# Batch 0 loaded in four row pieces and folded over d only; two thirds of the weight folding placed between FFN steps

## The chip, the cores and the metric

The kernel runs on one core of a Trainium2 chip. The time is the device time of a whole execution in microseconds (us). Runs of one kernel spread, and the profiled run is one of them (for the kernel before, it is one more, of 707.55 us).

Engine names in the profile: PE is TensorE, PEld its weight loads, DVE VectorE, ACT ScalarE, POOL GpSimd, SP the engine that issues most DMAs. "L434" is line 434 of that kernel's file, so the same instruction has another line number in another kernel.

## The reference

```python
def reference(x, w_gate, w_val, w_out):          # x (8, 3008, 256), weights 256 -> 1536 -> 256
    X = np.fft.fft(np.fft.fft(x, axis=1), axis=2).real.astype(np.float32)
    t = X.reshape(8 * 3008, 256)
    gate = np.maximum(t @ w_gate, 0.0)
    return (gate * (t @ w_val) @ w_out).astype(np.float32)
```

The kernel does the Fourier transform over the sequence in two matrix stages (3008 = 94 x 32) and puts the transform over d = 256 into the FFN weights ("weight fold": cosine and sine tables times the raw weights, 12 pieces of 512 columns, in fp32). Symmetry halves the work: rows j and 32-j, and columns d and 256-d, are first added and subtracted ("fold"), and the FFN of a mirrored position is had from the same products with one more term ("mirror").

The FFN is a chain of steps t = 0 to 287: 8 batches x 3 blocks x 12 column tiles f, 36 steps a batch. While the FFN of batch b runs, stage 1, a shuffle through DRAM, rotate and stage 2 of batch b+1, and load and fold of batch b+2, are slipped in at given steps.

## The kernel before

The load and the fold of one batch. A fold is a chain of small instructions on one engine; in the FFN loop GpSimd gets one of them per step (three in batch 0).

```python
def load_x(b, q):
    xl = xp.tile([NA, J, D], F32, tag="xl")             # one buffer each: the next load waits
    xh = xp.tile([96, NB // 2, D], F32, tag="xh")       # for the end of this fold
    for p0, n in ((0, 80), (80, 14)):
        q.dma_start(out=xl[p0:p0 + n], in_=...)
    nc.gpsimd.indirect_dma_start(out=xh[:]..., ...)     # the mirrored rows, gathered
...
def fold(b, eng, lo, hi):                               # chunks of up to 3 row pairs
    ...
    yield lambda: eng.tensor_tensor(c1, x1, rev, op=ALU.subtract)
    yield lambda: eng.tensor_tensor(x1, x1, rev, op=ALU.add)
    yield lambda: eng.tensor_tensor(e1[:, :, H + 1:D], ...)
    yield lambda: eng.tensor_tensor(e1[:, :, 1:H], ...)

def fold_all(b, eng):                                   # 23 fold steps
    for lo in range(1, J - 1, XC):
        yield from fold(b, eng, lo, min(lo + XC, J - 1))
    yield from fold_ends(b, eng)
    yield from fold_edges(b, eng, 0, J)                 # columns 0 and 128, once, at the end
```

The start: tables, the fold of batch 0 on DVE and GpSimd, stage 1, the shuffle, all weight folds, stage 2.

```python
load_x(0, nc.sync)
# ... the raw weights, 3 MB, in four loads right behind it; sine tables on DVE, ACT, POOL ...
for lo, hi in ((2, 5), (5, 8), (8, 10), (10, 12)):
    run(fold(0, nc.vector, lo, hi)); ...
for lo, hi in ((12, 14), (14, 16)):
    run(fold(0, nc.gpsimd, lo, hi))
...
for k, c in enumerate((1, 2, 3, 4, 5, 6, 7, 0)):
    stage1(0, c, "dve" if k in (5, 7) else "act")
for k in (2, 4, 6, 0):
    shuffle_out(0, k, k + 2)
load_x(1, nc.scalar)
...
for blk in range(NBLK):
    shuffle_in(0, 4 * blk, 4 * blk + 4)
run(fold_all(1, nc.gpsimd))
for n in range(DF // 512):
    for i in range(2):
        for cs in range(2):
            ...                                         # one weight fold: 2 fp32 matmuls 128x512 (psw)
rotate(0)
for blk in range(NBLK):
    stage2(0, blk, 0, "act"); stage2(0, blk, 1, "dve")
```

One FFN step. In a "split" step (two of three, from batch 1 on) the mirror product h is made by GpSimd, in the others by DVE. `gs` and `gm` share one pool of five buffers; GpSimd's mirror product is what frees `gm`. The names in the profiles: G and V are the gate and value products on TensorE, `gs` and `gm` the rectified gate of a position and of its mirror, E what DVE prepares for GpSimd's mirror product; `psw` is the product of a weight fold, `eo` the result of the fold, `pq` that of stage 2, `psr` that of rotate.

```python
gp = ctx.enter_context(tc.tile_pool(name="gp", bufs=5, space=SB))
def split(t):
    return NBLK * NF <= t < len(steps) and t % 3 != 2
...
def mirror_h(t, eng, val):
    eng.tensor_tensor(free(e["h"][:], ...), e["gm"][:]..., val[:]..., op=ALU.mult)
...
tl, tf, t1, tr, d2 = (17, 18, 16, 28, 1) if b == 0 else (1, 8, 6, 22, 2)   # load, fold, stage 1, rotate
```

## Time and profile before

| | before |
|---|---|
| time, median of 3 runs | 707.9 us (706.92 to 708.68) |
| span of the profiled run | 705.8 us |
| PE busy | 646.8 us (92%) |
| first G matmul of the FFN | 71.32 us |
| first gs ACTIVATE | 72.44 us |
| a step of batch 0: steps 0 to 11, 12 to 35 | 1.81, 2.42 us |
| a batch of 36 steps, batches 1 to 5 | 77.4 us |
| batch 6, which loads and folds nothing | 76.9 us |

A "batch" here is the time from the gs ACTIVATE of its first step to that of the next batch's first step.

First the chain of waits of the first 74 us: start, length, what. It names at each moment the work that everything later waited for.

```profile
1.73 18.37 DMA xh<-in_x_dram,ix
20.12 0.96 DVE xc L98
...
32.45 0.42 DVE xl L99
...
33.53 1.27 POOL xc L98
...
40.71 0.68 POOL eo L102
...
44.10 22.21 PE psw L346 x48
...
70.57 0.70 DVE pq L180
71.32 0.61 PE G L390
```

The start is one serial chain: 18 us for the gathered rows, DVE's fold, then GpSimd's two chunks alone until 41.4, stage 1, and 22 us of weight folding on TensorE. The shuffle of batch 0 is slow, too: the waits of the SP queue show (engine, line, for what: total, times, longest)

```profile
SPq L157 <- DMA Td<-t_282: 15.5, 1, 15.5
```

because it runs beside the loads of batch 1 and `w_out`. The Trainium skill ("DMA: Bandwidth & Descriptors", "Issuing engines are not separate DMA queues") says that DMAs of all issuing engines run on the same 16 DMA engines and interleave; the trace agrees: the wait was 15.5 us beside these loads. It cost nothing, as the weight fold hid it.

In the first 12 FFN steps TensorE has gaps. PE's part of the timeline, one step: start, duration, what, and in brackets the idle time before it and what ended that.

```profile
83.51 0.38 PE L434 MATMUL V<-pq,wm_91 128*128 128x512 bf16 x1 [0.37 <-DVE h L411]
83.72 0.38 PE L407 MATMUL V<-pq,wc_87 128*128 128x512 bf16 x1
83.94 0.38 PE L409 MATMUL V<-pq,ws_89 128*128 128x512 bf16 x1
84.16 0.38 PE L397 MATMUL G<-pq,wm_90 128*128 128x512 bf16 x1
84.37 0.38 PE L390 MATMUL G<-pq,wc_86 128*128 128x512 bf16 x1
84.58 0.38 PE L391 MATMUL G<-pq,ws_88 128*128 128x512 bf16 x1
85.33 0.38 PE L434 MATMUL V<-pq,wm_91 128*128 128x512 bf16 x1 [0.37 <-DVE h L411]
```

Six matmuls start 0.215 us apart and fill 1.29 us of a step of 1.82; the durations of 0.38 overlap. So each of these steps has 0.53 us of room. Later steps also carry the output matmuls, and TensorE is full: in batch 3 (busy time of each engine and number of instructions, windows view)

```profile
307.08:384.47 77.39, 76.46 (x516) 50.25 (x525) 62.78 (x97) 52.18 (x100) 59.97 (x49) 1.00 0.43 108
```

PE is busy 76.46 of 77.39 us; the columns after PE are PEld, DVE, ACT and POOL, then the clock, DMA share and GB/s.

### The profile page before, as it was taken

The numbers are of one execution on the slowest core, as the hardware profiler recorded it, in microseconds if no ns is written. First come the engines' busy times: TensorE is split into PE (matmuls) and PEld (weight loads), VectorE is DVE, ScalarE is ACT, GpSimd is POOL, SyncE is SP. The second block draws the span as 40 slices with busy tenths as digits, with TensorE's granted clock in tenths as the row PEclk, the third lists the DMA queues.
The fourth block names the chain that finished last, engine by engine and source line by source line (L and its number), as shares of the span: only waits on it lengthen the run. The fifth ranks groups of instructions, "written<-read, shape, count | busy, mean of one in ns | idle before, by whom it ended". The sixth has DMA issues, their size and how long they took to land.

```text
span 705.8 us, 12357 instructions
## 1 busy us (share of the span) xinstructions
PE 646.8 (92%) x4198; PEld 415.8 (59%) x4276; DVE 519.0 (74%) x830; ACT 428.5 (61%) x798; POOL 448.3 (64%) x393
## 2 busy tenths in 40 slices
PE   0169899899999999999999999999999999999997
PEld 0024356566666666666666666666666666666665
DVE  6712665568888878787888788888878888888881
ACT  2114557567666676667666766667676766665662
POOL 2845918915996499847995599747994334434341
PEclk9999999999999999999999999999999999999999
DMA  9458081573511932265413842185221151111213
GB/s 203 179 133 162 23 181 35 158 185 69 147 37 46 214 110 80 62 143 133 123 38 88 200 118 58 46 179 141 80 59 53 31 148 37 57 50 29 59 30 89
DMA packets 30480, 70.81 MB, mean 100 GB/s; under 512 B 4264, under 2 KB 21184, under 8 KB 28224
## 3 DMA queue, kind: packets, MB, share of 16 engines
q1 hardware_dynamic: 27844, 55.01, 29.6%
q0 software_dynamic: 2448, 13.37, 9.0%
q10 hardware_dynamic: 124, 1.64, 1.0%
q8 instruction: 33, 0.54, 0.3%
q14 instruction: 31, 0.25, 0.1%
HBM read 39.83 MB, written 30.96 MB: 100 GB/s over the span
## 4 chain that ended last, share of the span: by engine, by line
PE 72%; POOL 12%; issue 5%; DVE 4%; DMA 4%; ACT 1%; SPq 0%; DVEq 0%; POOLq 0%
PE po L452 28%; PE G L391 8%; PE V L409 7%; PE G L397 7%; PE V L407 6%; POOL h L423 6%; PE G L390 6%; PE V L434 3%; PE psw L346 3%; DMA xh<-in_x_dram,ix 3%; POOL xl L99 2%; POOL xc L98 2%; POOL eo L102 1%; DVE h L411 1%; POOL eo L100 1%
## 5 line engine op out<-in xcount | busy, mean ns | idle before, releaser
L423 POOL TENSOR_TENSOR h<-gm,E 128x512 bf16<-128x512 f32 x168 | 213.9, 1273 | 190.5 <-DVE E L431 169.9
L452 PE MATMUL po<-wo,h 128*128 128x256 bf16 x2304 | 324.2, 272 | 1.6
L452 PEld LDWEIGHTS <-h 128*128 128x128 bf16 x2304 | 222.6, 98 | 86.6 <-issue 10.8
L400 ACT ACTIVATE gm<-G 128x512 f32<-128x512 f32 x288 | 172.6, 599 | 140.1 <-PE G L397 140.1
L411 DVE TENSOR_TENSOR h<-gs,V 128x512 bf16<-128x512 f32 x288 | 190.3, 684 | 51.0 <-PE V L409 47.7
L392 ACT ACTIVATE gs<-G 128x512 f32<-128x512 f32 x288 | 171.8, 596 | 5.3 <-POOL h L423 3.0
L423 DVE TENSOR_TENSOR h<-gm,V 128x512 bf16<-128x512 f32 x120 | 82.6, 688 | 75.2 <-ACT gm L400 52.6
L417 DVE SCALAR_TENSOR_TENSOR E<-nb,af,V 128x512 f32<-128x512 bf16 x168 | 125.3, 746 | 7.0 <-PE V L407 3.6
L431 DVE SCALAR_TENSOR_TENSOR E<-E,V 128x512 f32<-128x512 f32 x168 | 114.3, 680 | 0.0
L397 PE MATMUL G<-pq,wm_90 128*128 128x512 bf16 x288 | 109.4, 380 | 2.2 <-ACT gs L392 2.1
L391 PE MATMUL G<-pq,ws_88 128*128 128x512 bf16 x287 | 109.0, 380 | 2.3
L409 PE MATMUL V<-pq,ws_89 128*128 128x512 bf16 x280 | 106.2, 379 | 0.1
L407 PE MATMUL V<-pq,wc_87 128*128 128x512 bf16 x263 | 100.0, 380 | 0.2 <-issue 0.2
L455 ACT COPY os<-po 128x512 f32<-128x512 f32 x96 | 56.2, 586 | 67.9 <-PE po L452 67.9
L390 PE MATMUL G<-pq,wc_86 128*128 128x512 bf16 x244 | 93.0, 381 | 0.8 <-DVE pq L180 0.8
L98 POOL TENSOR_TENSOR xc<-xl,xh 94x768 f32<-94x768 f32 (+1 forms) x37 | 66.0, 1784 | 34.7 <-DMA xh<-in_x_dram,ix 18.0
L99 POOL TENSOR_TENSOR xl<-xl,xh 94x768 f32<-94x768 f32 (+1 forms) x37 | 66.0, 1782 | 1.7
L434 PE MATMUL V<-pq,wm_91 128*128 128x512 bf16 x120 | 45.5, 379 | 3.9 <-DVE h L411 3.9
L409 PEld LDWEIGHTS <-ws_89 128*128 128x128 bf16 x288 | 28.2, 98 | 34.2 <-issue 0.3
L391 PEld LDWEIGHTS <-ws_88 128*128 128x128 bf16 x288 | 28.2, 98 | 34.0 <-issue 0.3
L134 PEld LDWEIGHTS <-w_81 94*96 94x96 bf16 x120 | 15.6, 131 | 50.1 <-issue 27.0
L407 PEld LDWEIGHTS <-wc_87 128*128 128x128 bf16 x288 | 28.2, 98 | 22.1 <-issue 7.5
(349 smaller groups left out, 393.7 us busy)
## 6 DMA issues: line engine op xcount, KB each, us to landing
out_dram<-os SPq DMA_DIRECT2D x176, 128.0 KB
xl<-in_x_dram SPq DMA_DIRECT2D x7, 1360.0 KB
nb<-Nd SPq DMA_DIRECT2D x24, 128.0 KB
xl<-in_x_dram SPq DMA_DIRECT2D x7, 238.0 KB
wst_108<-in_moe_w_gate_dram SPq DMA_DIRECT2D x2, 768.0 KB
wst_111<-in_moe_w_val_dram SPq DMA_DIRECT2D x2, 768.0 KB
out_dram<-os SPq DMA_DIRECT2D x16, 96.0 KB
xl<-in_x_dram ACTq DMA_DIRECT2D x1, 1360.0 KB
```

Source lines behind the costliest of these rows:

```text
L390: nc.tensor.matmul(e["G"][:], lhsT=wc[0][:, fs], rhs=pq[:, 0, :], start=True, stop=False)
L391: nc.tensor.matmul(e["G"][:], lhsT=ws[0][:, fs], rhs=pq[:, 1, :], start=False, stop=True)
L392: nc.scalar.activation(e["gs"][:], e["G"][:], ACTF.Relu)
L397: nc.tensor.matmul(e["G"][:], lhsT=wm[0][:, f * 128:(f + 1) * 128], rhs=pqt[b, blk][:, 1, :], start=False, stop=True, skip_group_check=True)
L400: nc.scalar.activation(e["gm"][:], e["G"][:], ACTF.Relu)
L407: nc.tensor.matmul(e["V"][:], lhsT=wc[1][:, fs], rhs=pq[:, 0, :], start=True, stop=split(t))
L409: nc.tensor.matmul(e["V"][:], lhsT=ws[1][:, fs], rhs=pq[:, 1, :], start=False, stop=True, skip_group_check=split(t))
L411: nc.vector.tensor_tensor(e["h"][:, 0, :], e["gs"][:], e["V"][:], op=ALU.mult)
L417: nc.vector.scalar_tensor_tensor(e["E"][:], nbt[b, blk][:], af[:, f:f + 1], e["V"][:], op0=ALU.mult, op1=ALU.add)
L423: eng.tensor_tensor(free(e["h"][:], 512 + NB - 1, [NB, 16], [-1, NB]), e["gm"][:].rearrange("p (a k) -> p a k", k=NB), val[:].rearrange("p ...
L431: nc.vector.scalar_tensor_tensor(e["E"][:], e["E"][:], 2.0, e["V"][:], op0=ALU.mult, op1=ALU.subtract)
L452: nc.tensor.matmul(po[:, s % 2, :], lhsT=ht[t - f + ff]["h"][:, sg, g * 128:(g + 1) * 128], rhs=wo[:, ff, :], start=(ff == 0), stop=(ff == ...
```

## The change

Intent: shorten the start. Batch 0 comes in four row pieces on one queue, alone; each piece is folded over d as soon as it is there, and the mirrored rows are not added by DVE but by a second matmul in stage 1, with its own table `w1h`. The raw weights come in thirds, into buffers that `h` uses later; one third is folded before the FFN, the others at steps 0 to 7, where TensorE has room. The loads of batch 1 are issued after the shuffle. Because batch 1 comes later, the plan of loads, folds and stages moved, and GpSimd's mirror products start 8 steps later.

```diff
+    FIRST = (0, 24, 8, 16)
+    def load_first():
+        ...
+        for r in FIRST:
+            nc.sync.dma_start(out=(xl if r < 16 else xh)[:, r % 16:r % 16 + 8, :],
+                              in_=view(x, r * D, [[NB * D, 96], [1, 8 * D]]))
+    def fold_first(r):                       # over d only: two tensor_tensors of 94 x 8 x 127, one copy
+        ...
     def stage1(b, c, evac):
...
-            if jj:
+            if jj and b == 0:
+                nc.tensor.matmul(o, lhsT=w1[:, jj, :], rhs=eo[:, jj, :], start=True, stop=False)
+                nc.tensor.matmul(o, lhsT=w1h[:, NB // 2 - jj, :], rhs=eh[:, NB // 2 - jj, :], start=False, stop=True)
+            elif jj:
...
     def fold(b, eng):                        # now 22 fold steps
...
+            eng.tensor_copy(free(e1, 0, [D, n], [H, 2]), free(x1, 0, [D, n], [H, 2]))   # edges, in each chunk
...
-        yield from fold_edges(b, eng, 0, J)
...
+        for blk in range(NBLK):
+            shuffle_in(0, 4 * blk, 4 * blk + 4)
+        load_w(1)
+        load_w(2)
...
+        nc.gpsimd.tensor_copy(si[0:1, 0:1], wst[1, 2, 1][0:1, 0:1])   # holds batch 1's gather back
+        load_x(1, nc.sync)
...
+        for i in range(2):
+            for cs in range(2):
+                fold_w(0, i, cs)
...
-        return NBLK * NF <= t < len(steps) and t % 3 != 2
+        return NBLK * NF + 8 <= t < len(steps) and t % 3 != 2
...
+    for k in range(4):
+        at(k, fold_w, 1, k // 2, k % 2)
+        at(4 + k, fold_w, 2, k // 2, k % 2)
+        at(8 + k, stage2, 0, 1 + k // 2, k % 2, "dve")
+    # load, fold, stage 1, shuffle, rotate, stage 2
+    plan = {0: (28, 34, (14, 16, 18, 19, 21, 23, 24, 25), 26, 33, (33, 34, 36, 38, 40, 42)),
+            1: (12, 19, range(11, 19), 19, 26, (26, 27, 29, 31, 33, 35)),
+            2: (7, 13, range(6, 14), 14, 22, (23, 25, 27, 29, 31, 33))}
...
-            for fn in itertools.islice(folds[0], 3 if t < NBLK * NF else 1):
+        for k in range(2 if t < NBLK * NF + 8 else 1):
+            while folds and next(folds[0], folds) is folds:
```

## The prediction

> **What bounds it now.** Two regimes. From the end of the prologue on, TensorE is the limit: the windows view gives PE busy 197.4 us in 200:400 and 197.8 in 400:600 at clock 1.00, and successive gs ACTIVATEs are 2.15 us apart on average. Before that is a serial prologue of 71.3 us (first G matmul in the timeline at 71.32). The chain of waits through it: the gather of xh lands at 20.1 (18.4 us, beside xl and the 3 MB of raw weights); DVE folds to 33.3; POOL folds alone 33.5 to 41.5; stage 1 ends at 44.1; the 48 fp32 weight-fold instructions hold PE to 66.3 (22.2 us; the first four 0.85 us each, then 0.43); stage 2 and its evictions to 71.3.
>
> **What the change does.**
> - Batch 0 arrives as four 0.79 MB pieces, alone at first. At the 190 to 260 GB/s of the first microseconds I estimate landings near 5.5, 9, 12.5 and 16 us.
> - DVE builds a table twice as wide (94x1536; from 1.00 us for a 94x816 tensor_tensor I estimate 1.9, all of it done near 8 us), then folds each piece in two tensor_tensors of 94x1016 (about 1.1 us each, from 0.4 per 381 elements) plus edges: 2.5 us a piece, last done near 18.5. The row fold (and POOL's 8 us) is gone; 15 extra 94x256 matmuls come, about 0.2 us each.
> - Stage 1 then ends near 23.5 and the shuffle is no longer behind batch 1's loads. Now shuffle_in waits 15.5 us for it (waits of the SP queue), hidden under the weight fold. The Trainium skill, "DMA: Bandwidth & Descriptors", section on issuing engines, says queues interleave on the same 16 engines; the trace agrees, and the change issues batch 1's load after the shuffle. I expect t4 near 31.
> - One third of the weight fold stays: 16 instructions, about 8.5 us with the cold start, near 25.5 to 34. First gs near 37.5 instead of 72.4: 35 us saved.
> - Given back: 8 folds of 1.72 us between steps 0 to 7. These steps take 1.82 us now with 6 matmuls of 0.215, so 0.5 us of each is PE slack; with the fold they become PE-bound at 3.0. Steps 8 to 11 carry stage 2, about 2.1. Block of 12: 32.5 instead of 21.7 us, +10.8.
> - Steps 36 to 43 become unsplit (6 value/gate matmuls, 2.4 against 2.16 us) and take stage 2 of batch 1: +2.5. The 4.2 us step of batch 0 (rotate waiting for its DMA) should vanish: -1.5. POOL's backlog near step 44, where the mirror products start behind fold 2: +0.5.
>
> **Sum.** 707.9 - 35 + 10.8 + 2.5 - 1.5 + 0.5 = about 685 us (-3.2%). Range 679 to 692. Faster by over 2% 0.93, within 2% 0.06, slower 0.01.
>
> **What would show it.** First gs at 35 to 40 us; wait of stage 1 on the last piece, not on POOL; steps 0 to 7 at about 3.0 us with PE busy throughout; steps 12 to 35 near 2.35 us; unchanged 2.15 us in batches 2 to 7.
>
> **What would make it wrong.** The pieces landing late (then the first gs slips one for one); shuffle_in taking much more than 5 us; the raw weights of the other thirds landing after steps 0 to 4 need them; batch 1's fold on POOL (from near 55 us, 29 us long) arriving late for stage 1 at step 14; a POOL backlog at step 44 that stalls E and gs buffers for several us.

## The result

| | before | after |
|---|---|---|
| time, median (4 runs each) | 708.06 us | 690.98 us (690.47 to 693.31) |
| ratio, 95% interval | | 0.9767 (0.9741 to 0.9793) |
| span of the profiled run | 705.8 us | 688.8 us |
| PE busy | 646.8 us (92%) | 653.0 us (95%) |
| first gs ACTIVATE | 72.44 us | 36.56 us |

Ratios are the mean time of one kernel's fast runs over the mean of the other's of the same rounds, so not quite the ratio of the medians.

The change is 17 us faster. Lengths of the batches, worked out from the start times of the gs ACTIVATEs in the two timelines:

| us | first gs | batch 0 | 1 | 2 | 3 | 4 | 5 | 6 |
|---|---|---|---|---|---|---|---|---|
| before | 72.44 | 79.82 | 77.41 | 77.41 | 77.39 | 77.42 | 77.41 | 76.93 |
| after | 36.56 | 87.49 | 80.42 | 79.83 | 79.57 | 78.72 | 79.61 | 76.93 |
| difference | -35.9 | +7.7 | +3.0 | +2.4 | +2.2 | +1.3 | +2.2 | 0 |

The start brings 35.9 us. Batch 0 gives back 7.7, which was foreseen (weight folds between steps). But batches 1 to 5 give back another 11.1, and 8.1 of these, in batches 2 to 5, nobody had asked for: the FFN work there is the same.

The start, after, from the timeline: the fold of the last piece, the weight folds, the first FFN matmul, the first gs.

```profile
15.79 2.41 DVE L130 TENSOR_TENSOR eo<-xh 94x1016 bf16<-94x1016 f32 x3 [0.50 <-DMA xh<-in_x_dram]
22.20 0.58 ACT L171 CAST t_168<-ps_214 96x512 bf16<-96x512 f32 x1 [0.27 <-PE ps_214 L159]
23.59 8.99 PE L251 MATMUL psw<-wst,cd 128*128 128x512 f32 x16 [1.42 <-ACT cd L281]
34.31 0.38 PE L432 MATMUL G<-pq,wc_103 128*128 128x512 bf16 x1 [1.00 <-ACT pq L206]
36.56 0.60 ACT L434 ACTIVATE gs<-G 128x512 f32<-128x512 f32 x1 [2.30 <-POOL si L399]
```

DVE waits 0.50 us for the last piece, stage 1 is evicted by 22.8 (44.8 before), the weight folds are 16 instructions and 9.0 us instead of 48 and 22.2, and the first G matmul is at 34.31 instead of 71.32.

Now the loss. Page part 5, the gs group of both kernels (busy us, mean ns, then the idle time before it and its main cause), before and after:

```profile
L392 ACT ACTIVATE gs<-G 128x512 f32<-128x512 f32 x288 | 171.8, 596 | 5.3 <-POOL h L423 3.0
```

```profile
L434 ACT ACTIVATE gs<-G 128x512 f32<-128x512 f32 x288 | 171.6, 596 | 15.0 <-POOL h L465 12.6
```

gs waits four times as long for GpSimd's mirror products, and TensorE then waits for gs. In the stretch from 230 to 640 us the waits view has, before,

```profile
ACT gs L392 <- POOL h L423: 2.4, 4, 0.6
PE G L397 <- ACT gs L392: 1.7, 4, 0.4
```

and after

```profile
ACT gs L434 <- POOL h L465: 11.9, 15, 1.2
PE G L439 <- ACT gs L434: 7.9, 11, 1.0
POOL xc L99 <- DMA xh<-in_x_dram,ix: 2.6, 3, 1.0
```

(before, no `xc` waits for DMA there). GpSimd's total is no larger: in batch 3, after,

```profile
284.30:363.87 79.57, 77.24 (x526) 50.23 (x525) 62.86 (x97) 52.52 (x100) 60.40 (x54) 1.00 0.41 105
```

POOL is busy 60.40 us where it was 59.97. But it is crowded: GpSimd's timeline at the beginning of that fold has

```profile
314.78 1.27 POOL L465 TENSOR_TENSOR h<-gm,E 128x512 bf16<-128x512 f32 x1 [3.75 <-DVE E L473]
316.97 1.81 POOL L99 TENSOR_TENSOR xc<-xl,xh 94x768 f32<-94x768 f32 x1 [0.92 <-DMA xh<-in_x_dram,ix]
318.74 1.27 POOL L465 TENSOR_TENSOR h<-gm,E 128x512 bf16<-128x512 f32 x1
319.96 1.82 POOL L100 TENSOR_TENSOR xl<-xl,xh 94x768 f32<-94x768 f32 x1
321.73 1.00 POOL L101 TENSOR_TENSOR eo<-xc 94x381 bf16<-94x381 f32 x1
...
323.90 0.22 POOL L103 CAST eo<-xl 94x6 bf16<-94x6 f32 x1
```

and from there no idle time until the fold ends at 364. The windows view of the fold stretch, before and after, has GpSimd in the last column of the engines:

```profile
327.14:374.20 47.06, 46.34 (x315) 30.38 (x320) 37.71 (x60) 31.98 (x61) 46.32 (x38) 1.00 0.27 77
```

```profile
316.97:364.00 47.03, 44.70 (x307) 28.67 (x305) 36.55 (x57) 29.77 (x56) 46.78 (x42) 1.00 0.23 66
```

Both hold one whole fold and 14 mirror products, and GpSimd is busy for nearly all of either. Before, a fold is dealt out over 23 FFN steps, which last 49.2 us at batch 6's pace (76.93 / 36 = 2.137 us a step); after, over 22 steps, which last 47.0.

An estimate of what GpSimd owes in these steps: by the durations, the fold of a batch is five chunks of 1.81 + 1.81 + 1.00 + 0.99, two ends of 0.71 and six edge copies of 0.2, together 30.7 us, dealt out over 22 FFN steps; mirror products add 2/3 x 1.27 = 0.85 us a step, 18.6 us in 22 steps. That would be 49.3 us, 2.3 us more than there is, and this is the figure in the expectations below. But the durations overlap a little: from the start of one to the start of the next without a gap, a mirror product takes 1.23 us, not 1.27. Counted so, it is 29.8 + 18.1 = 47.9 us of work in 47.0 after, and 29.3 + 18.9 = 48.2 us in 49.2 before: 0.9 us short now, 0.9 us to spare then. The work is not even, either: the 20 steps that hold the five chunks alone owe 44.7 us and have 42.7, and the light steps for the ends come last. (Before, these 20 steps owed 44.1, and a batch with a fold took about 0.5 us longer than batch 6.)

The other loss is at two single steps. In batch 0, step 33 takes 3.80 us, and in batch 1, step 62 takes 4.26. The timeline around step 33, after:

```profile
115.55 0.18 PE L191 MATMUL psr<-t_1058,rot 128*128 128x12 bf16 x1
115.76 0.69 DVE L465 TENSOR_TENSOR h<-gm,V 128x512 bf16<-128x512 f32 x1 [1.26 <-PE psr L191]
116.37 0.68 DVE L453 TENSOR_TENSOR h<-gs,V 128x512 bf16<-128x512 f32 x1
116.96 0.20 DVE L192 CAST t_1058<-psr 128x12 bf16<-128x12 f32 x1
117.22 0.38 PE L203 MATMUL ps_1242<-m_100,t_1058 128*128 128x128 bf16 x4 [1.49 <-DVE t_1058 L192]
```

The plan puts rotate and the first stage 2 into the same step. Stage 2 needs DVE's copy of the rotated column, DVE has two h products to do first, and TensorE stands still for 1.49 us.

### The profile page after: what moved, and what is told of

It reads as the page before. It is cut to its first block, busy times and chain, and to the rows that moved or that the text cites. A ratio compares the mean times of both kernels' runs of the same rounds, so it can differ in the third digit from the quotient of the medians.

```text
span 688.8 us, 12467 instructions
## 1 busy us (share of the span) xinstructions
PE 653.0 (95%) x4297; PEld 419.5 (61%) x4297; DVE 508.5 (74%) x800; ACT 436.2 (63%) x811; POOL 424.1 (62%) x398
## 4 chain that ended last, share of the span: by engine, by line
PE 61%; POOL 18%; DMA 10%; issue 5%; DVE 2%; ACT 2%; SPq 1%; POOLq 0%; DVEq 0%
PE po L494 24%; PE V L451 7%; POOL h L465 7%; PE G L439 6%; PE G L432 6%; PE G L433 6%; PE V L449 6%; DMA xl<-in_x_dram 5%; POOL xl L100 4%; POOL xc L99 4%; PE V L476 3%; DMA xh<-in_x_dram,ix 3%; DMA xh<-in_x_dram 2%; PE psw L251 2%; POOL eo L101 2%
## 5 line engine op out<-in xcount | busy, mean ns | idle before, releaser
L465 POOL TENSOR_TENSOR h<-gm,E 128x512 bf16<-128x512 f32 x162 | 205.9, 1271 | 166.6 <-DVE E L473 166.0
L465 DVE TENSOR_TENSOR h<-gm,V 128x512 bf16<-128x512 f32 x126 | 86.7, 688 | 85.6 <-ACT gm L442 60.8
L459 DVE SCALAR_TENSOR_TENSOR E<-nb,af,V 128x512 f32<-128x512 bf16 x162 | 120.8, 746 | 6.6 <-PE V L449 6.1
L439 PE MATMUL G<-pq,wm_107 128*128 128x512 bf16 x288 | 109.1, 379 | 9.9 <-ACT gs L434 9.5
L473 DVE SCALAR_TENSOR_TENSOR E<-E,V 128x512 f32<-128x512 f32 x162 | 110.2, 680 | 0.0
L432 PE MATMUL G<-pq,wc_103 128*128 128x512 bf16 x288 | 109.1, 379 | 1.0 <-ACT pq L206 1.0
L449 PE MATMUL V<-pq,wc_104 128*128 128x512 bf16 x288 | 109.1, 379 | 0.0
L433 PE MATMUL G<-pq,ws_105 128*128 128x512 bf16 x288 | 109.1, 379 | 0.0
L451 PE MATMUL V<-pq,ws_106 128*128 128x512 bf16 x288 | 109.0, 379 | 0.0
L99 POOL TENSOR_TENSOR xc<-xl,xh 94x768 f32<-94x768 f32 x35 | 63.4, 1811 | 50.0 <-DMA xl<-in_x_dram 34.1
L100 POOL TENSOR_TENSOR xl<-xl,xh 94x768 f32<-94x768 f32 x35 | 63.4, 1812 | 1.6
L433 PEld LDWEIGHTS <-ws_105 128*128 128x128 bf16 x288 | 28.1, 98 | 35.0 <-issue 1.1
L451 PEld LDWEIGHTS <-ws_106 128*128 128x128 bf16 x288 | 28.1, 98 | 34.2 <-DVE ws_106 L256 0.4
L476 PE MATMUL V<-pq,wm_108 128*128 128x512 bf16 x126 | 47.7, 379 | 0.3
L432 PEld LDWEIGHTS <-wc_103 128*128 128x128 bf16 x288 | 28.1, 98 | 18.6 <-issue 15.6
L449 PEld LDWEIGHTS <-wc_104 128*128 128x128 bf16 x288 | 28.2, 98 | 17.6 <-issue 1.3
```

The costliest lines, as they stand in the source:

```text
L432: nc.tensor.matmul(e["G"][:], lhsT=wc[0][:, fs], rhs=pq[:, 0, :], start=True, stop=False)
L433: nc.tensor.matmul(e["G"][:], lhsT=ws[0][:, fs], rhs=pq[:, 1, :], start=False, stop=True)
L439: nc.tensor.matmul(e["G"][:], lhsT=wm[0][:, f * 128:(f + 1) * 128], rhs=pqt[b, blk][:, 1, :], start=False, stop=True, skip_group_check=True)
L449: nc.tensor.matmul(e["V"][:], lhsT=wc[1][:, fs], rhs=pq[:, 0, :], start=True, stop=split(t))
L451: nc.tensor.matmul(e["V"][:], lhsT=ws[1][:, fs], rhs=pq[:, 1, :], start=False, stop=True, skip_group_check=split(t))
L459: nc.vector.scalar_tensor_tensor(e["E"][:], nbt[b, blk][:], af[:, f:f + 1], e["V"][:], op0=ALU.mult, op1=ALU.add)
```

## The experiments

Three theories for batches 2 to 5: A, GpSimd is overfull in the fold stretch; B, the rows of x land after their first fold step is due and block GpSimd, whose timelines keep the order of the program; C, TensorE itself is slowed by where stages 1 and 2 now stand. Besides these, what each part of the change is worth. Twelve kernels ran, all gave a right result. Their batches, worked out from their timelines as above:

| us | first gs | batch 0 | 1 | 2 | 3 | 4 | 5 | 6 |
|---|---|---|---|---|---|---|---|---|
| changed kernel again | 38.09 | 89.17 | 81.03 | 79.97 | 79.15 | 78.65 | 79.63 | 76.93 |
| e1 edges once | 36.90 | 97.53 | 81.96 | 80.24 | 78.65 | 78.33 | 79.12 | 76.94 |
| e2 load earlier | 37.20 | 87.47 | 80.45 | 79.13 | 78.62 | 78.63 | 78.64 | 76.94 |
| e3 slower fold | 37.70 | 87.47 | 80.63 | 81.80 | 76.93 | 76.96 | 76.94 | 76.94 |
| e4 waiting copy | 36.48 | 88.46 | 80.10 | 79.90 | 78.96 | 78.76 | 80.12 | 76.94 |
| e5 weights first | 49.08 | 78.14 | 80.92 | 79.52 | 78.62 | 78.87 | 79.21 | 76.94 |
| e6 old first load | 52.73 | 88.45 | 80.48 | 79.98 | 79.08 | 78.94 | 78.98 | 76.94 |
| e7 rotate earlier | 37.72 | 85.84 | 83.04 | 80.70 | 79.28 | 78.59 | 79.36 | 76.94 |
| e8 rotate and pace | 39.07 | 85.84 | 79.25 | 81.51 | 79.78 | 76.97 | 76.93 | 76.93 |
| e9 longer gap | 37.24 | 85.84 | 78.86 | 77.91 | 78.16 | 76.74 | 76.94 | 76.93 |
| e10 more buffers | 37.39 | 87.48 | 80.47 | 76.93 | 77.43 | 77.30 | 77.22 | 76.93 |
| e11 both | 39.59 | 85.85 | 79.03 | 77.88 | 78.21 | 76.96 | 76.93 | 76.94 |

Times of the runs are given with each. The first gs of kernels with the same start lies between 36.5 and 39.6 us in the profiled runs; differences of a microsecond there mean nothing.

### a0: the changed kernel again

> The changed kernel itself, once more, for a comparison in the same rounds: 690 to 692, ratio 0.975 to 0.978, batches 2 to 5 at 78.6 to 80.2 us each.

Measured: 691.13 us, ratio 0.9753 (0.9736 to 0.9769). Batches 2 to 5 lie within 0.4 us of the first profile; so do the waits of gs for GpSimd from 230 to 640 us (11.6 us against 11.9). The loss of the later batches is a property of the kernel. The profiled run was the slowest of the five (694.09).

### e1: the edge copies once, at the end

```diff
-            eng.tensor_copy(free(e1, 0, [D, n], [H, 2]), free(x1, 0, [D, n], [H, 2]))
-        ends = free(xl[0:NA], 0, [(J - 1) * D, 2], [H, 2])
-        eng.tensor_copy(free(eo[:], 0, [(J - 1) * D, 2], [H, 2]), ends)
...
+        yield eng.tensor_copy(free(eo[:], 0, [D, J], [H, 2]), free(xl[0:NA], 0, [D, J], [H, 2]))
```

> The changed kernel with the edge copies of the row fold taken out of each chunk and done once at the end, as its own 23rd fold step (before, they were done so). Theory A (GpSimd is overfull in the fold stretch of batches 2 to 5: 22 fold steps plus mirror products need about 50 us in the 47 us that 22 FFN steps last, so mirror products come late and the gate buffers run out): 0.8 us less GpSimd work and one step more room per batch, each of batches 2 to 5 goes from about 79.5 us to about 78.2, total 686 to 688. Rival B (the rows of x land too late for the first fold step and block GpSimd): no change, within 1 us of 691. Rival C (the loss is TensorE's, from where stage 1 and 2 stand): no change.

Measured: 701.59 us, ratio 0.991 (0.989 to 0.993): 10 us slower than the change, which no theory had. The waits of that kernel in steps 12 to 18 tell why:

```profile
PE ps L159 <- POOL eo L108: 8.6, 1, 8.6
```

Stage 1 of batch 1 starts at step 14, with the first chunk, while GpSimd still folds the last ones. If the edges of all chunks are copied at the very end, stage 1 waits for the end (step 14 takes 12.4 us). So the extra copies that the change makes are the price of starting stage 1 chunk by chunk. For the question asked, batches 3 to 5 are fit, where the fold ends long before stage 1: they are 0.9, 0.4 and 0.5 us shorter than in the first profile of the change. That is the direction of A and under half of its size. Inconclusive taken alone.

### e2: x loaded two steps earlier

```diff
-            2: (7, 13, range(6, 14), ...
+            2: (5, 13, range(6, 14), ...
```

> The changed kernel with the load of x two steps earlier in batches 2 to 5 (step 5 instead of 7), the fold where it was. Rival B (late x): each of batches 2 to 5 loses its 2 us of stalls, total 682 to 685. Theory A (GpSimd overfull): GpSimd's first wait of about 1 us goes, its overload stays; less than 3 us gained, total 688 to 691.

Measured: 688.66 us, ratio 0.9722 (0.97 to 0.9744). The waits of GpSimd's fold for DMA are gone from 230 to 640 us, and gs still waits 8.8 us for mirror products there (11.9 in the change):

```profile
ACT gs L434 <- POOL h L465: 8.8, 12, 1.0
```

Batches 3 to 5 take 78.6 us, 1.7 above batch 6. Late x is real and the smaller part (the four batches are 2.7 us shorter together, of the 8.1 lost); B does not explain the rest.

### e3: the same fold, spread over 26 steps

```diff
-            2: (7, 13, range(6, 14), ...
+            2: (4, 10, range(6, 14), ...
...
-        for k in range(2 if t < NBLK * NF + 8 else 1):
+        for k in range(2 if t < NBLK * NF + 8 else 0 if t >= 2 * NBLK * NF and t % 6 == 5 else 1):
```

> The changed kernel with load and fold of batches 2 to 5 three steps earlier (steps 4 and 10, the same gap of 6) and no fold step in every sixth FFN step, so that the 22 fold steps spread over 26 FFN steps. Same work. Theory A: waits of the gs ACTIVATE on GpSimd's h fall from 12.6 us to under 3 in batches 2 to 7, batches 2 to 5 take about 77.3 us each, total 682 to 684. Rival B: the gap is the same, so x is as late: 689 to 691. Rival C: no change.

Measured: 687.13 us, ratio 0.9696 (0.9672 to 0.972). Batches 3, 4 and 5 take 76.93, 76.96 and 76.94 us: exactly batch 6, which folds nothing, and better than before the change. Batch 3 in the windows view:

```profile
287.60:364.53 76.93, 76.40 (x516) 50.19 (x525) 62.86 (x97) 52.09 (x99) 60.39 (x54) 1.00 0.44 109
```

POOL's work is the same (60.39 us against 60.40), stages 1 and 2 stand where they stood, the gap from load to fold is the same six steps. The pace differs: 30.7 / 26.4 + 0.85 = 2.01 us a step (1.95 from start to start), under 2.137. This rules out C for these three batches. Against B it does not speak alone, as x came in time in these three batches too; but in e2 x came in time at the old pace, and 1.7 us a batch remained. Together they leave A as the larger cause and B as the smaller. The total misses the 682 to 684 expected, for batch 2 got worse (81.80): its load at step 76 comes while GpSimd still folds batch 3 from the one x buffer, so x is late for the first fold step. The waits view of 230 to 640 us has it:

```profile
POOL xc L99 <- DMA xl<-in_x_dram: 4.5, 1, 4.5
```

### e10: seven gate buffers

If late mirror products stop TensorE only through the five buffers of gs and gm, two more should do as much as a slower fold.

```diff
-    gp = ctx.enter_context(tc.tile_pool(name="gp", bufs=5, space=SB))
+    gp = ctx.enter_context(tc.tile_pool(name="gp", bufs=7, space=SB))
```

> The changed kernel with seven gate buffers (gs, gm) instead of five, nothing else. In batches 2 to 5 the fold stretch gives GpSimd 30.7 us of fold and 22 x 0.85 us of mirror products in 22 steps that TensorE could do in 47.0: an overload of about 2.3 us, and x is late by 1 to 2 us on top. Two more buffers let TensorE run one more step (2.1 us) ahead of GpSimd. If late mirror products hold up TensorE only through these buffers: batches 2 to 5 fall from about 79.4 to 77 to 78 us each, total 682 to 686. Rival (E's three buffers or h bind as well): under 2 us gained.

Measured: 682.65 us, ratio 0.9648 (0.9626 to 0.9669); batches 2 to 5 take 76.9 to 77.4 us. The waits view from 230 to 640 us:

```profile
ACT gs L434 <- POOL h L465: 2.2, 4, 0.8
PE G L439 <- ACT gs L434: 0.5, 2, 0.3
```

11.9 became 2.2, 7.9 became 0.5. GpSimd has the same work in the same steps; its lateness only no longer stops TensorE. The Trainium skill ("Perfetto Trace Analysis", "Optimization Strategy") says that the same gap repeating on the engine that should be saturated can mean that there is not enough memory for the next tile, naming buffer count; here two more buffers took most of the gap away, though e3 did so without them.

### e4: the waiting copy writes elsewhere

The first gs waits 2.30 us for GpSimd's one-element copy, which waits for the last raw weights: the pool of gs lies on memory of the setup pool, in which that copy has its target.

```diff
-        nc.gpsimd.tensor_copy(si[0:1, 0:1], wst[1, 2, 1][0:1, 0:1])
+        nc.gpsimd.tensor_copy(tick[:], wst[1, 2, 1][0:1, 0:1])
```

> The changed kernel with the one-element GpSimd copy, which waits for the last raw weights, writing to a tile of its own instead of one in the setup pool. The pool of gs lies on the setup pool's memory, so the first gs waits for that copy (2.3 us in the trace). Theory: first gs 1.5 us earlier, at about 35; TensorE idle 0.7 us less, total 0.5 to 1.5 us less (689.5 to 690.5). Rival (the wait is filled, TensorE has the weight fold to do meanwhile): first gs earlier, total within 0.3 us.

Measured: 690.65 us, ratio 0.9748 (0.9727 to 0.9769), beside 0.9753 for the change itself in other rounds. In the trace gs now follows its matmul, but step 0 is longer (3.05 us instead of 1.55); TensorE had its weight fold to do meanwhile. The first gs itself was no earlier (36.48 against 36.56), because in that run the G matmul before it came 1.5 us later. So the wait of 2.3 us cost nothing that these runs can see, as the rival has it; with intervals of 1.5 us either way, a gain of 0.5 us can't be excluded.

### e5 and e6: one part of the change at a time

e5 keeps the piecewise load and folds all weights before the FFN:

```diff
-        for i in range(2):
-            for cs in range(2):
-                fold_w(0, i, cs)
+        for n in range(3):
+            for i in range(2):
+                for cs in range(2):
+                    fold_w(n, i, cs)
...
-        at(k, fold_w, 1, k // 2, k % 2)
-        at(4 + k, fold_w, 2, k // 2, k % 2)
```

> The changed kernel with all 12 weight folds ahead of the first FFN step, none between steps; the piecewise load of batch 0 stays. If weight folds between steps cost what TensorE has no room for and save only its idle time (0.53 us of each 1.82 us step): first gs later by 8 x 1.72 = 13.7 us, at about 50; the first 12 steps 21.7 us again instead of 30.9; total about 4.5 us above the changed kernel, 695 to 696. Rival (the folds between steps delay the FFN by more than they take): total at or under 691.

Measured: 693.56 us, ratio 0.9798 (0.9778 to 0.9818). First gs at 49.08, 12.5 us later; the first 12 steps 21.5 us instead of 30.9, 9.3 us less. The difference is 3.2 us, near the 4.5 expected (in medians 2.4 us). Moving 13.7 us of TensorE work out of the start brought 3.2 us, no more than TensorE had free in the FFN (8 x 0.53 = 4.2 us).

e6 keeps the weight folds between steps and loads batch 0 as before, in one load and a gather, with the fold over rows on DVE and GpSimd:

```diff
-    load_first()
+    load_x(0, nc.sync)
...
-        for r in FIRST:
-            fold_first(r)
+        for lo, hi in ((2, 5), (5, 8), (8, 10), (10, 12)):
+            fold_old(nc.vector, lo, hi)
+        for lo, hi in ((12, 14), (14, 16)):
+            fold_old(nc.gpsimd, lo, hi)
...
-            if jj and b == 0:
-                ... (two matmuls)
-            elif jj:
+            if jj:
```

> The changed kernel with batch 0 loaded by one row load and the gather, folded over rows too on DVE and GpSimd as before; the weight folds between steps stay. If the piecewise load is what brings most: stage 1 ends near 40 again, the shuffle after it is then not hidden by anything, first gs at 52 to 56, total 707 to 711, no gain over before left. Rival (moving the weight folds is the main gain): total under 700.

Measured: 706.66 us, ratio 0.9973 (0.9949 to 0.9998). First gs at 52.73. Its chain of waits begins

```profile
1.70 16.91 DMA xh<-in_x_dram,ix
18.64 0.97 DVE xc L146
```

so the fold cannot begin before 18.6, where the changed kernel has the last piece folded at 18.3. The piecewise load, with the fold over d only that it allows, is worth 16.2 us at the first gs (52.73 to 36.56) and about 15.7 us of the total, and without it the change as it stands would have gained almost nothing, since its later batches cost 11 us. It is not that the rest of the new start is worthless: against before, e6 has its first gs 19.7 us earlier, about 14 of them from the moved weight folds (an estimate: 32 instructions of 0.43 us). The rest was not taken apart; the trace shows the gather at 16.9 us instead of 18.4, and GpSimd folding its chunks beside DVE instead of after its table work.

### e7: rotate a step earlier

```diff
-            ... 26, 33, (33, 34, 36, ...
-            ... 19, 26, (26, 27, 29, ...
+            ... 26, 32, (33, 34, 36, ...
+            ... 19, 25, (26, 27, 29, ...
```

> The changed kernel with the rotate of batches 1 and 2 one FFN step ahead of the first stage 2 (steps 32 and 61) instead of in the same step. In the trace TensorE waits 1.49 us at each of the two, because stage 2 needs DVE's copy of the rotated column, which stands in DVE's queue behind two h products. Expected: steps of 3.80 and 4.26 us become about 2.3 and 2.7, total 3 us less, about 688. Rival (filled by later slack): under 1 us.

Measured: 690.35 us, ratio 0.9734 (0.9717 to 0.9752). Step 33 fell from 3.80 to 2.13 us, as expected, and batch 0 from 87.5 to 85.8. Batch 1 did not gain: in the profiled run step 61 takes 6.01 us, with

```profile
PE psr L191 <- DMA t<-Td: 2.4, 1, 2.4
```

Rotate now came before its data. In that run one group of output stores held the SP queue for 7.45 us (1.73 in e8), and the shuffle behind it went out late. The profiled run was the slowest of five (692.94; the others 689.16 to 690.44), so this is not in every run. So about half of the expected 3 us is shown in batch 0; in the totals it lies within the noise (the intervals of e7 and a0 overlap).

### e8 and e9: both mends

e8 has e7's rotate, the slower pace from step 44 on, and other steps for load and fold:

```diff
+            2: (9, 15, range(6, 14), ...
+            3: (6, 12, range(6, 14), ...
+            4: (4, 10, range(6, 14), ...
```

> The changed kernel with both mends: rotate one step earlier, and no fold step in every sixth FFN step from step 44 on, with loads and folds moved so that x and the buffer are there (load and fold at 9 and 15 in batch 2, 6 and 12 in batch 3, 4 and 10 after). If GpSimd's overload explains all of what batches 2 to 5 lost, each takes 76.9 us, as batch 6, which folds nothing; batch 1 about 77.5 to 78; batch 0 about 86; total 675 to 678.

Measured: 687.3 us, ratio 0.9697 (0.968 to 0.9714). Batches 4 and 5 reach 76.9, batches 2 and 3 do not (81.5, 79.8). SP's waits show that the load of batch 4 was held back 7.1 us until GpSimd had finished with the x buffer:

```profile
SPq L82 <- POOL eo L108: 7.1, 1, 7.1
```

and the first fold step started 17.9 us after that load was issued (225.07 to 242.92 in the timeline), later than the plan's 6 steps. GpSimd stood idle 5.2 us before it, and the mirror products stood behind it. (The view puts this wait down to DVE; the gather of these rows, issued at 225.20, took 17.6 us to land, which is the same moment.) The 76.9 I expected for all four batches took no account of that.

e9 puts 7 to 9 steps between load and fold, and in batch 1 moves stage 2 a step later instead of rotate a step earlier:

```diff
+            1: (12, 19, range(11, 19), 19, 26, (27, 28, 29, 31, 33, 35)),
+            2: (10, 19, range(6, 14), ...
+            3: (10, 18, range(6, 14), ...
+            4: (8, 16, range(6, 14), ...
+            5: (7, 14, range(6, 14), ...
```

> The changed kernel with the rotate a step ahead of stage 2 in batches 0 and 1 (in batch 1 by moving the first stage 2 pieces a step later, as step 61 was too early for the shuffle), no fold step in every sixth FFN step from step 44 on, and 7 to 9 steps between the load of x and its fold (10 and 19 in batch 2, 10 and 18, 8 and 16, 7 and 14 after). If what stayed in e8 was x landing after its fold step and blocking GpSimd, batches 2 to 5 all take 76.9 to 77.3 us, batch 0 86, batch 1 77.5 to 79.5; total 678 to 681, faster than both kernels. Rival (the load now collides with the shuffle, both late): no better than e8, 686 to 688.

Measured: 680.98 us, ratio 0.9604 (0.9585 to 0.9623): 28 us faster than before, 10 us faster than the change (ratio 0.9753 in the same rounds). Batches 2 to 5: 77.9, 78.2, 76.7, 76.9. In batches 2 and 3 step 22 takes 1 us more, because the load now runs beside the shuffle, and from the issue of the shuffle's write to that of its read 13.1 and 13.8 us pass (6.4 and 6.6 in the change):

```profile
PE psr L191 <- DMA t<-Td: 0.8, 1, 0.8
```

### e11: e9 with seven gate buffers

> The kernel of e9 with seven gate buffers too. In e9 step 22 of batches 2 and 3 still takes 1 us more (rotate waits for a shuffle that the load of x slowed), which buffers can't mend; GpSimd no longer binds there. So at most 1 us less than e9: 679 to 681.

Measured: 680.35 us, ratio 0.9612 (0.9589 to 0.9634), the same as e9. Once the pace is right, more buffers bring nothing: the two mends cure one cause.

## Why the prediction was right, and where its sum was off

The forecast was 685 us (679 to 692) and the measurement 690.98: inside the range, near its upper end; 17 us gained where 23 were forecast. That the total stays inside is partly luck: the term that failed alone is worth 8.1 us, more than the 7 us between 685 and the end of the range, and the start and the weight folds came out 2.6 us better than forecast. Term by term:

| term of the prediction | predicted | measured | |
|---|---|---|---|
| first gs | -35 | -35.9 | right |
| steps 0 to 11, weight folds | +10.8 | +9.1 | about right; steps 0 to 7 took 2.97 us each |
| rest of batch 0 | -1.5 | -1.5 | the sum is right, the step is not |
| batch 1 (+2.5, +0.5) | +3.0 | +3.0 | right by accident |
| batches 2 to 5 ("unchanged 2.15 us") | 0 | +8.1 | wrong |

- **The start.** The last two pieces landed as estimated (DVE waited for them until 12.84 and 15.79 us, where 12.5 and 16 had been forecast), stage 1 ended at 22.8 instead of 23.5, the weight folds at 32.6 instead of 34. E5 and e6 confirm the two parts: 3 us for the weight folds between steps, 16 us at the first gs for the pieces.
- **The rotate.** The 4.2 us step of before did vanish, but I had not seen that the new plan puts rotate and stage 2 in one step twice. That stall cost about 1.6 us in batch 0 (e7), and about as much in batch 1: step 62 took 4.26 us, and 2.39 in e9, where rotate has a step of its own.
- **Batch 1.** I gave the eight unsplit steps 2.5 us, from 2.4 us a step; but that pace of before included stage 1. Steps 36 to 47 cost 0.85 us more. What made up for it was the stalled step 62.
- **Batches 2 to 5.** "Unchanged 2.15 us in batches 2 to 7" is the term that failed. I saw that the work was the same and only moved, and looked for a backlog of GpSimd at step 44, but did not add up GpSimd's work per step in the later folds. Six edge copies in place of one, and one fold step fewer, turned an estimated 48.2 us of work in 49.2 us into 47.9 in 47.0; and the fold comes six steps after the load where seven had just been enough. E3, read with e2, shows the pace to be the larger cause, e10 shows that the five gate buffers are how it reaches TensorE, e2 shows the share of late x. The sizes of the two are not cleanly split: the estimate for the pace alone (0.9 us a batch on the average of the fold stretch, 2.0 by the end of its five chunks) and e2's remainder (1.7 us) are not the same thing.

What stays open: why the first gs varies by 3 us between profiled runs of the same start, and the last 2 us of batch 1 over batch 6, of which the eight unsplit steps should be part.

## What to carry to other kernels

When a change moves deferred work of an engine that is "only 62% busy" (GpSimd on the changed kernel's page), divide that work by the steps in which it must be done and add what the engine owes in every step; an average over the span hides a stretch of 47 us without a gap. Work in a slow, in-order queue should be dealt out over all the steps that its deadline allows, and its data should be there with a margin, for one late operand delays everything behind it. Here, moving work from an idle start into a busy loop bought no more than the loop's idle time (e5), while shortening the first load and what hangs on it came through almost in full (e6: 16.2 us at the first gs, 15.7 in the total).

## What the Trainium skill lacked or had wrong

- "ScalarE: Activation LUTs" ("What ACT_TABLE_LOAD costs") gives 2.66 us for a switch of tables, 1.28 for the load and 1.38 for a drain. In the changed kernel Abs ends at 8.73, the load runs from 8.76 for 1.28 us, and the next Sin starts at 10.05: 1.3 us in all, no drain to be seen. The page also says ("Table sets: the hidden batching unit") that abs is in every table set; an Abs after Sin, at 22.68, indeed needs no load. But the Abs that comes first in the program got a table of its own, and the first Sin a second load. The page does not warn that a cheap function ahead of the first expensive one can cost a load (here off the critical path).
- "Perfetto Trace Analysis" ("Optimization Strategy") names too few buffers as a reason for repeating gaps, and e10 agrees (11.9 us of waits to 2.2). It does not name the other way that worked here, to spread the late engine's work over more steps without more memory: 76.93 us a batch in e3, 76.93 to 77.43 with more buffers.
